# A backward pass of attention and MLP: the weight gradient of the output projection first, and weight and dQ transposes moved into the dw2 stage

## The chip, the cores and the metric

The kernel runs on one core of one Trainium2 chip. The metric is device time in microseconds (us) of one execution; medians of several executions are given, with the number of them.

## The reference, cut to what matters

The reference is the forward pass of a block and its gradients for 2048 rows of width 512, in bf16. The forward pass is `x + s * g`, where `s` is attention (32 heads of width 16) on the normalised `x`, and `g` is `silu` of an MLP of inner width 1792 on the same input.

```python
xn = _layernorm(x, axis=-1)
s = _A_ref(xn, A_wqkv, A_wo)                       # qkv, softmax attention, @ wo
g = _silu(_B_ref(xn, B_w1, B_b1, B_w2, B_b2))      # layernorm, gelu MLP
return x + s * g
# ... reference(): the output, and the vjp for x, wqkv, wo, w1, b1, w2, b2
```

The change touches only the weight gradients that follow the attention backward pass: `dwo` (512x512), `dwqkv` (512x1536, in a q, a k and a v third) and `dw2` (1792x512), with the output projection (attention's output times `wo`), which the forward output needs and which gives `dm`, the gradient that `dw2` and the MLP go on from.

## The kernel before: the parts that matter

The kernel computes attention forward and backward until its last matmul, called Z, at about 2223 us. Then comes the stretch below. Two queues issue its DMAs: `nc.sync` (the SP queue) carries all the transposing DMAs and the stores of the output, `nc.scalar` (the ACT queue) the plain loads. The instructions are ordered by a scheduler: what the program says first need not be issued first, when it is ready and its buffer is free.

```python
# ... pools: c4 has 5 buffers (oT, dKVn and dso share them), psA 7 PSUM banks
load_oT(0); load_oT(1)                  # SP queue: transposes of attention's output
load_gbx(0); load_gbx(1)                # ACT queue: gb (256 KB) and xt (128 KB) of a row tile, 3 buffers each
for i in range(4):
    nc.scalar.dma_start(out=xn_all[...], in_=xnv[...])            # 4 x 512 KB
load_oT(2); load_oT(3)
for i in range(4):
    nc.sync.dma_start_transpose(out=dQT[...], in_=k.dQall[...])   # needed only after dw2
# ...
for t in range(NT):                     # 16 row tiles: projection, and q third of dwqkv
    # 4 matmuls ps_so = oT @ wo
    nc.vector.tensor_tensor(out=dm_all[:, t, :], in0=ps[:], in1=gb[:, 1, :], op=ALU.mult)
    # t13 = ps * gb[0]; ot = t13 + xt
    if t + 2 < NT:
        load_gbx(t + 2)
    # store of ot (SP queue), 4 matmuls ps_dwq (q third), every second t a transpose of dm_all (SP queue)
    if t == 1:
        load_kv(0)                      # SP queue: dKVn, one of 8 transposes for the k and v thirds
    if t in (4, 6, 8, 10):
        load_kv(t // 2 - 1)
    if t == 5:
        load_hg(k.HGT_s, 0)             # SP queue: hgc, first of 7 transposes for dw2, 2 buffers
    if t == 9:
        nc.sync.dma_start_transpose(out=w2T[:], in_=B_w2)         # needed only after dw2
    if t == 11:
        load_hg(k.HGT_s, 1)
    if t == 13:
        nc.sync.dma_start_transpose(out=w1T[:], in_=B_w1)         # needed only after dw2
# ...
for half in range(2):                   # k and v thirds of dwqkv: 2 x 64 matmuls from dKVn
    # ...
    load_kv(i + 5)                      # while any is left, then dso (ACT queue, 512 KB each)
# psdb: 16 small matmuls; then dwo: 64 matmuls ps_dwo = Oall^T @ dso
y_all = k.pO.tile([128, NT, D], bf16, name="y_all", tag="slotA")  # Oall's place, so after dwo
nc.scalar.dma_start(out=y_all[:], in_=...)                        # 2 MB
for i in range(3):
    load_gp(i)                          # ACT queue, 896 KB each, needed after dw2
for i in range(7):                      # dw2: 224 matmuls ps_dw from hgc and dm_all
    # ...
    if i + 2 < 7:
        load_hg(k.HGT_s, i + 2)
# ... then dhg (it needs w2T and gp) and the rest
```

Of the kernel before, what the change touches and what calls it, by code (L numbers as in the profile page):

```python
# [8 lines left out]
bf16 = mybir.dt.bfloat16  # L9
f32 = mybir.dt.float32  # L10
# [5 lines left out]
S, D, H, DH, F = 2048, 512, 32, 16, 1792  # L16
NT = S // 128
IC = D // 128
# [254 lines left out]
def phase3(ctx, tc, k, A_x, A_wqkv, A_wo, B_w1, B_w2, grad_out, out_0, out_1, out_2, out_3, out_4, out_5, out_6, out_7, dbg):  # L273
    nc = tc.nc
# [4 lines left out]
    with ExitStack() as c1:  # L279
# [23 lines left out]
        with ExitStack() as c2:  # L303
# [27 lines left out]
            def dwq_out(half, ps4):  # L331
                for ic in range(IC):
                    ob = ring.tile([128, D], bf16, name="dw_out", bufs=3)
                    nc.scalar.copy(out=ob[:], in_=ps4[ic][:])
                    nc.scalar.dma_start(out=out_2[ic * 128:(ic + 1) * 128, half * D:(half + 1) * D], in_=ob[:])

            load_oT(0)
            load_oT(1)
            load_gbx(0)
            load_gbx(1)  # L340
            xnv = k.XN_s.rearrange("(t p) d -> p t d", p=128)
            for i in range(4):
                nc.scalar.dma_start(out=xn_all[:, 4 * i:4 * i + 4, :], in_=xnv[:, 4 * i:4 * i + 4, :])
            load_oT(2)
            load_oT(3)
            for i in range(4):
                nc.sync.dma_start_transpose(out=dQT[:, 4 * i:4 * i + 4].rearrange("c t m q -> c (t m) q"),
                                            in_=k.dQall[:, 4 * i:4 * i + 4, :].rearrange("q t c -> q (t c)"))
            psdb2 = psS.tile([1, D], f32, name="psdb2")
            acc4 = [psA.tile([128, D], f32, name="ps_dwq", tag="mm") for _ in range(IC)]  # L350
            ots = {}
# [7 lines left out]
            for t in range(NT):  # L359
                ps = psA.tile([128, D], f32, name="ps_so", tag="mm")  # L360
                for cc in range(IC):
                    nc.tensor.matmul(ps[:], lhsT=oT[t // 4][:, t % 4, cc, :], rhs=wo_sb[:, cc, :],
                                     start=(cc == 0), stop=(cc == IC - 1))
                gb, xt = gbx.pop(t)
                nc.vector.tensor_tensor(out=dm_all[:, t, :], in0=ps[:], in1=gb[:, 1, :], op=ALU.mult)
                t1 = wk.tile([128, D], f32, name="t13")
                nc.vector.tensor_tensor(out=t1[:], in0=ps[:], in1=gb[:, 0, :], op=ALU.mult)
                ot = wk.tile([128, D], bf16, name="ot3", bufs=4)
                nc.gpsimd.tensor_tensor(out=ot[:], in0=t1[:], in1=xt[:], op=ALU.add)
                ots[t] = ot  # L370
                if t + 2 < NT:
                    load_gbx(t + 2)
                if t >= 2:
                    store_o0(t - 2)
                for ic in range(IC):
                    nc.tensor.matmul(acc4[ic][:], lhsT=xn_all[:, t, ic * 128:(ic + 1) * 128], rhs=k.dQall[:, t, :],
                                     start=(t == 0), stop=(t == NT - 1))
                if t % 2 == 0 and t >= 2:
                    dmT_tr(t // 2 - 1)
                if t == 1:  # L380
                    load_kv(0)
                if t in (4, 6, 8, 10):
                    load_kv(t // 2 - 1)
                if t == 5:
                    load_hg(k.HGT_s, 0)
                if t == 9:
                    nc.sync.dma_start_transpose(out=w2T[:], in_=B_w2)
                if t == 11:
                    load_hg(k.HGT_s, 1)
                if t == 13:  # L390
                    nc.sync.dma_start_transpose(out=w1T[:], in_=B_w1)
            store_o0(NT - 2)
            store_o0(NT - 1)
            dmT_tr(NT // 2 - 1)
            dwq_out(0, acc4)
            dso = {}

            def load_dso(i):
                dso[i] = c4.tile([128, 4, D], bf16, name="dso3", tag="c4")
                nc.scalar.dma_start(out=dso[i][:], in_=k.DSO_s[i * 512:(i + 1) * 512, :].rearrange("(t p) d -> p t d", p=128))  # L400

            for half in range(2):
                acc4 = [psA.tile([128, D], f32, name="ps_dwq", tag="mm") for _ in range(IC)]
                for t4 in range(4):
                    i = half * 4 + t4
                    for ic in range(IC):
                        for tt in range(4):
                            t = t4 * 4 + tt
                            nc.tensor.matmul(acc4[ic][:], lhsT=xn_all[:, t, ic * 128:(ic + 1) * 128], rhs=kvc[i][:, tt, :],
                                             start=(t == 0), stop=(t == NT - 1))  # L410
                    if i + 5 < 8:
                        load_kv(i + 5)
                    else:
                        load_dso(i + 5 - 8) if i + 5 - 8 < 4 else None
                dwq_out(half + 1, acc4)
            for t in range(NT):
                nc.tensor.matmul(psdb2[0:1, :], lhsT=k.ones_bf[:, 0:1], rhs=dm_all[:, t, :], start=(t == 0), stop=(t == NT - 1))
            db2 = wk.tile([1, D], bf16, name="db2", bufs=1)
            nc.vector.tensor_copy(out=db2[:], in_=psdb2[:])
            nc.sync.dma_start(out=out_7.rearrange("(o d) -> o d", o=1), in_=db2[:])  # L420
            acc4 = [psA.tile([128, D], f32, name="ps_dwo", tag="mm") for _ in range(IC)]
            for t4 in range(4):
                for ac in range(IC):
                    for tt in range(4):
                        t = t4 * 4 + tt
                        nc.tensor.matmul(acc4[ac][:], lhsT=k.Oall[:, t, ac * 128:(ac + 1) * 128], rhs=dso[t4][:, tt, :],
                                         start=(t == 0), stop=(t == NT - 1))
            for ac in range(IC):
                dwo = ring.tile([128, D], bf16, name="dw_out", bufs=3)
                nc.scalar.copy(out=dwo[:], in_=acc4[ac][:])  # L430
                nc.sync.dma_start(out=out_3[ac * 128:(ac + 1) * 128, :], in_=dwo[:])
            y_all = k.pO.tile([128, NT, D], bf16, name="y_all", tag="slotA")
            nc.scalar.dma_start(out=y_all[:], in_=k.Y_s.rearrange("(t p) d -> p t d", p=128))
            dxm_all = k.pO.tile([128, NT, D], bf16, name="dxm_all", tag="slotB")
            for i in range(3):
                load_gp(i)
            for i in range(7):
                for fl in range(2):
                    fc = 2 * i + fl
                    ps = psA.tile([128, D], f32, name="ps_dw2", tag="mm")  # L440
                    for t in range(NT):
                        nc.tensor.matmul(ps[:], lhsT=hgcs[i][:, t, fl * 128:(fl + 1) * 128], rhs=dm_all[:, t, :], start=(t == 0), stop=(t == NT - 1))  # L442
                    dw2 = ring.tile([128, D], bf16, name="dw_out", bufs=3)
                    nc.scalar.copy(out=dw2[:], in_=ps[:])
                    nc.scalar.dma_start(out=out_6[fc * 128:(fc + 1) * 128, :], in_=dw2[:])
                if i + 2 < 7:
                    load_hg(k.HGT_s, i + 2)
            R = [big.tile([128, 8, S // 2], bf16, name="R0", tag="s16a")]
            Rv = k.dKVT_s.rearrange("(r p) s -> p r s", p=128)
            nc.scalar.dma_start(out=R[0][:], in_=Rv[:, :, 0:S // 2])  # L450
# [571 lines left out]
```

## Time and profile before

| | before |
|---|---|
| time, median of 3 executions | 2628.93 us (2627.68 to 2630.96) |
| span of the profiled execution | 2624.7 us |
| last Z matmul (end of attention) | 2222.6 us |
| first dw2 matmul | 2367.6 us |
| last dw2 matmul | 2418.0 us |
| from there to the end | 206.7 us |

The page of the profile gives the busy time of the engines over the whole span:

```profile
PE 2295.2 (87%) x18152; PEld 731.6 (28%) x18192; DVE 1837.6 (70%) x3286; ACT 1673.4 (64%) x1910; POOL 908.0 (35%) x1391
```

An average of 87% hides the stretch of the change. The view of busy times by stretches shows it, cut at the stage borders of this kernel. Its columns are start and end, the length, the busy time of each engine with its instructions in brackets, and last the granted TensorE clock, the DMA share and GB/s.

```profile
core 0: us, PE busy (x) PEld busy (x) DVE busy (x) ACT busy (x) POOL busy (x), PEclk, DMA share, GB/s
2223.00:2243.40 20.40, 0.00 (x0) 0.01 (x1) 0.66 (x1) 0.00 (x0) 0.61 (x1) 0.58 1.07 308
2243.40:2305.90 62.50, 36.95 (x126) 14.53 (x130) 17.85 (x29) 1.07 (x2) 13.75 (x12) 0.80 1.17 259
2305.90:2353.80 47.90, 36.14 (x142) 14.97 (x145) 3.36 (x5) 5.22 (x9) 4.61 (x4) 0.80 0.96 230
2353.80:2367.60 13.80, 13.75 (x65) 6.22 (x65) 0.00 (x0) 2.39 (x5) 0.00 (x0) 1.00 0.15 50
2367.60:2418.20 50.60, 48.62 (x221) 21.73 (x225) 0.00 (x0) 8.19 (x14) 0.00 (x0) 1.00 0.76 186
```

The lines are: PE without work; projection and q third; k and v thirds; dwo; dw2. In the first three the DMA share is about 1 (a share of 1 is 16 busy engines; the records overlap a little, so it can exceed 1) and PE waits for half of the time. In the last two PE is busy throughout, and the DMA engines have room: their share is 0.76 in dw2 and 0.15 in dwo.

The waits of PE and of VectorE in the same stretch (us in total, number, longest):

```profile
PE ps_so L362 <- DVE t L367: 21.4, 6, 7.4
PE ps_so L362 <- DMA gb<-GB_s: 20.5, 1, 20.5
PE ps_dwq L409 <- DMA dKVn<-dKVT_s: 11.6, 1, 11.6
...
DVE dm_all L365 <- DMA gb<-GB_s: 37.1, 9, 8.0
```

The second line is the first 20 us. The waits of the projection for VectorE are at one remove waits for DMA too: VectorE itself waits 37 us for `gb` loads. And the kv matmuls wait once, 11.6 us, for a `dKVn` transpose. The timeline shows which one (start, length, engine, line; in brackets the idle time before and what ended it):

```profile
2333.97 8.41 SPq L320 DMA_TRANSPOSE dKVn<-dKVT_s  x3
...
2341.23 12.71 PE L409 MATMUL ps_dwq<-dKVn,xn_all 128*128 128x512 bf16 x47 [11.60 <-DMA dKVn<-dKVT_s]
2353.78 13.98 PE L426 MATMUL ps_dwo<-dso,Oall 128*128 128x512 bf16 x63
2367.59 13.98 PE L442 MATMUL ps_dw<-dm_all,hgc 128*128 128x512 bf16 x63
```

The last `dKVn` transposes are issued from 2334 to 2342.4. From there on PE runs without a wait, through the rest of the kv matmuls and dwo into dw2. So the stretch has two parts. Until the last `dKVn`, 119.8 us after the last Z, the DMA engines bound it; in the 25.2 us from there to dw2, PE does.

### The profile page before, as it was taken

How to read it: one execution, taken by the hardware profiler on the slowest of the kernel's cores; microseconds unless marked ns; L12 is line 12 of the kernel's file. 1: busy time of each engine (PE TensorE's matmuls, PEld its weight loads, DVE VectorE, ACT ScalarE, POOL GpSimd, SP SyncE). 2: the span in 40 equal slices, each digit the busy share in tenths (PEclk: the TensorE clock that was granted, in tenths of full speed). 3: DMA queues.
4: the chain of work that ended last, by engine and by line, in shares of the span. 5: the costliest groups of instructions: out<-in, count | busy, mean ns of one | idle time of the engine just before them, and what ended most of it. 6: DMA issues, size and time to landing. Idle time of an engine off the chain costs nothing.

```text
span 2624.7 us, 47762 instructions
## 1 busy us (share of the span) xinstructions
PE 2295.2 (87%) x18152; PEld 731.6 (28%) x18192; DVE 1837.6 (70%) x3286; ACT 1673.4 (64%) x1910; POOL 908.0 (35%) x1391
## 2 busy tenths in 40 slices
PE   3788699999999999999999899999999997479998
PEld 2333122222222222222222222222222222134446
DVE  5766578887778878788878778888888885201652
ACT  3344578777777877788777777777777775011141
POOL 0533545454535445454445454521101111100020
PEclk8899799999999999999999999999999999789999
DMA  5355899999999999999999999999999998987475
GB/s 192 92 184 184 179 239 232 236 236 234 226 236 237 237 231 237 231 234 242 231 235 233 237 228 240 235 236 233 226 233 229 236 218 183 271 215 186 153 160 125
DMA packets 1905432, 568.51 MB, mean 217 GB/s; under 512 B 1811889, under 2 KB 1887794, under 8 KB 1905202
## 3 DMA queue, kind: packets, MB, share of 16 engines
q1 hardware_dynamic: 1844674, 511.05, 95.8%
q10 hardware_dynamic: 60528, 54.41, 6.7%
q8 instruction: 142, 2.33, 0.4%
q14 instruction: 88, 0.72, 0.1%
HBM read 52.83 MB, written 62.66 MB: 44 GB/s over the span
## 4 chain that ended last, share of the span: by engine, by line
PE 38%; DVE 33%; issue 12%; DMA 10%; ACT 4%; POOL 2%; SPq 0%; ACTq 0%; DVEq 0%; POOLq 0%
DVE gts L743 26%; PE d L708 6%; PE X L789 6%; PE Z L858 4%; DMA gk<-gts 4%; PE Z L852 3%; PE t L680 3%; PE X L774 2%; PE ps_dhg L463 2%; DVE xs L795 2%; ACT et L722 2%; DVE xt L807 2%; PE XT L805 1%; PE ps_dw L528 1%; PE ps_dw L442 1%
## 5 line engine op out<-in xcount | busy, mean ns | idle before, releaser
L743 DVE TENSOR_TENSOR gts<-d,et 128x512 bf16<-128x512 f32 x2048 | 1302.5, 682 | 359.1 <-issue 240.8
L722 ACT ACTIVATE et<-s 128x1024 bf16<-128x1024 f32 x1024 | 1002.6, 1024 | 24.9 <-PE d L708 13.8
L730 ACT ACTIVATE e<-t 128x1024 bf16<-128x1024 f32 x512 | 523.8, 1023 | 407.3 <-PE t L680 405.7
L708 PE MATMUL d<-QDT,KVT 32*128 32x512 bf16 x2048 | 599.1, 383 | 130.9 <-DVE gts L743 129.5
L694 PE MATMUL s<-QDT,KVT 32*128 32x512 bf16 x2048 | 403.3, 390 | 18.2 <-DMA QDT<-QDPad 11.9
L774 PE MATMUL X<-et,Lc 128*32 128x512 bf16 x2048 | 403.9, 391 | 14.1 <-DVE xs L795 14.1
L777 PE MATMUL X<-et,NAT 128*32 128x512 bf16 x2048 | 403.9, 391 | 0.0
L789 PE MATMUL X<-gts,NAT 128*17 128x512 bf16 x2048 | 402.5, 389 | 0.0
L858 PE MATMUL Z<-gk,W 128*32 128x512 bf16 x2048 | 399.4, 384 | 0.0
L822 POOL TENSOR_TENSOR W<-NATQd,rL 128x128 bf16<-128x128 bf16 x64 | 25.7, 402 | 645.9 <-DVE rL L817 645.9
L789 PEld LDWEIGHTS <-NAT 128*17 128x17 bf16 x2048 | 92.5, 87 | 492.0 <-issue 492.0
L852 PE MATMUL Z<-e,W 128*32 128x512 bf16 x1024 | 202.2, 388 | 3.8 <-DVE acc L865 2.3
L852 PE MATMUL Z<-ek,W 128*32 128x512 bf16 x1024 | 203.7, 394 | 0.0
L680 PE MATMUL t<-KVT,QDT 32*128 32x512 bf16 x1024 | 201.0, 389 | 0.0
L694 PEld LDWEIGHTS <-KVT 32*128 32x128 bf16 x2048 | 97.4, 91 | 362.6 <-issue 362.5
L708 PEld LDWEIGHTS <-KVT 32*128 32x128 bf16 x2048 | 139.0, 91 | 88.9 <-issue 59.6
L774 PEld LDWEIGHTS <-Lc 128*32 128x32 bf16 x2048 | 103.7, 93 | 180.4 <-issue 179.4
L865 DVE TENSOR_TENSOR acc<-Z,acc 64x512 f32<-64x512 f32 x192 | 129.2, 673 | 12.2 <-PE Z L858 12.2
L852 PEld LDWEIGHTS <-W 128*32 128x32 bf16 x2048 | 121.1, 93 | 56.7 <-issue 50.2
L777 PEld LDWEIGHTS <-NAT 128*32 128x32 bf16 x2048 | 101.2, 96 | 52.2 <-issue 2.7
L631 POOL TENSOR_TENSOR bg_v<-bg_t 128x512 f32<-128x512 f32 x56 | 58.1, 1038 | 149.1 <-ACT bg_t L638 149.1
L870 POOL CAST ob<-acc 64x512 bf16<-64x512 f32 x64 | 38.6, 603 | 203.3 <-DVE acc L865 203.3
(161 smaller groups left out, 2525.8 us busy)
## 6 DMA issues: line engine op xcount, KB each, us to landing
gk<-gts SPq DMA_TRANSPOSE x512, 4.1
HGT_s<-hgT SPq DMA_DIRECT2D x2, 3584.0 KB, 12.2
bg_x<-H1T_s SPq DMA_DIRECT2D x56, 128.0 KB, 2.8
GP_s<-bg_m SPq DMA_DIRECT2D x56, 128.0 KB, 2.5
gp<-GP_s ACTq DMA_DIRECT2D x8, 896.0 KB, 8.5
DH1T_s<-dh1T SPq DMA_DIRECT2D x4, 1792.0 KB, 10.2
NAT<-NAT_s SPq DMA_DIRECT2D x16, 264.0 KB, 3.2
GB_s<-gB ACTq DMA_DIRECT2D x16, 256.0 KB, 2.0
```

What stands on the lines that cost most here:

```text
L680: nc.tensor.matmul(t[:, hj, :], lhsT=op["QDT"][r:r + 32, q0:q0 + 128], rhs=op["KVT"][r:r + 32, kc * 512:(kc + 1) * 512], start=True, stop= ...
L694: nc.tensor.matmul(s[:, hj, :], lhsT=op["KVT"][r:r + 32, kb * 128:(kb + 1) * 128], rhs=op["QDT"][r:r + 32, qc * 512:(qc + 1) * 512], start ...
L708: nc.tensor.matmul(d[:], lhsT=op["KVT"][r:r + 32, kb * 128:(kb + 1) * 128], rhs=op["QDT"][r:r + 32, qc * 512:(qc + 1) * 512], start=True, ...
L722: nc.scalar.activation(out=et[:, :, kb % 4, :, :].rearrange("k b h q -> k h b q"), in_=st_s.pop(g)[:].rearrange("k h (b q) -> k h b q", b= ...
L730: nc.scalar.activation(out=e[:], in_=st_t.pop(g)[:], func=ACT.Exp)
L743: nc.vector.tensor_tensor(out=gts[:, kb % 2, hj, :].rearrange("k (b q) -> k b q", b=4), in0=ds[hj][:].rearrange("k (b q) -> k b q", b=4), ...
L774: nc.tensor.matmul(X[64 + 32 * hj:96 + 32 * hj, :], lhsT=Lc[:], rhs=et[:, :, kb % 4, hj, :], start=(kb == 0), stop=False, skip_group_check ...
L777: nc.tensor.matmul(X[32 * hj:32 * hj + 32, :], lhsT=NATt[:, kb, hj, 1:33], rhs=et[:, :, kb % 4, hj, :], start=(kb == 0), stop=(kb == 15), ...
L789: nc.tensor.matmul(X[64 + 32 * hj:64 + 32 * hj + 17, :], lhsT=NATt[:, kb, hj, 0:17], rhs=gts[:, kb % 2, hj, :], start=False, stop=(kb == 1 ...
L852: nc.tensor.matmul(Z[32 * hj:32 * hj + 32, :], lhsT=blk[j]["W1"][:, qb, hj, :], rhs=ev[:, hj], start=(qb == qb_order[0]), stop=False, tile ...
L858: nc.tensor.matmul(Z[32 * hj:32 * hj + 32, :], lhsT=blk[j]["W2"][:, qb, hj, :], rhs=gv[:, :, :, hj, qb, :], start=False, stop=(qb == qb_or ...
L865: nc.vector.tensor_tensor(out=av, in0=Z[0:64, :], in1=av, op=ALU.add)
```

## The change

The change has two halves. First, dwo needs only what attention left (`Oall`) and `dso`, so it is put ahead of the projection, into the time in which PE has nothing to do, and its 14 us vanish from the PE-bound end. Secondly, the transposes of `w2`, `w1` and dQ, which are not needed before dw2 ends, go into the dw2 stage, whose DMA engines have room. `HGT` transposes, for dw2, go into the k and v thirds. No matmul is added or dropped.

```diff
+            load_dso(0)
+            load_dso(1)
+            load_dso(2)
             load_oT(0)
             load_oT(1)
             load_gbx(0)
             load_gbx(1)
+            load_dso(3)
+            load_oT(2)
             # ... xn_all loads
-            load_oT(2)
+            acc4 = [psA.tile([128, D], f32, name="ps_dwo", tag="mm") for _ in range(IC)]
+            # ... dwo: 64 matmuls, 4 copies out, 4 stores (moved here, stores on the ACT queue)
             load_oT(3)
-            for i in range(4):
-                nc.sync.dma_start_transpose(out=dQT[...], in_=k.dQall[...])
+            load_kv(0)
             # ... projection, q third
-                if t == 1:
-                    load_kv(0)
-                if t in (4, 6, 8, 10):
-                    load_kv(t // 2 - 1)
-                if t == 5:
-                    load_hg(k.HGT_s, 0)
-                if t == 9:
-                    nc.sync.dma_start_transpose(out=w2T[:], in_=B_w2)
-                if t == 11:
-                    load_hg(k.HGT_s, 1)
-                if t == 13:
-                    nc.sync.dma_start_transpose(out=w1T[:], in_=B_w1)
+                if t in (8, 9, 12, 15):
+                    load_kv({8: 1, 9: 2, 12: 3, 15: 4}[t])
             # ... k and v thirds
-                    else:
-                        load_dso(i + 5 - 8) if i + 5 - 8 < 4 else None
+                    if i == 2:
+                        load_hg(k.HGT_s, 0)
+                    if i == 4:
+                        load_hg(k.HGT_s, 1)
             # ... psdb
-            # ... dwo (moved to the front)
             y_all = k.pO.tile([128, NT, D], bf16, name="y_all", tag="slotA")
             # ... y_all and gp loads, dw2 loop
                 if i + 2 < 7:
                     load_hg(k.HGT_s, i + 2)
+                if i == 1:
+                    nc.sync.dma_start_transpose(out=w2T[:], in_=B_w2)
+                if i == 3:
+                    nc.sync.dma_start_transpose(out=w1T[:], in_=B_w1)
+                if i >= 4 and i < 6:
+                    # ... two of the four dQT transposes
```

More of the change, by code (lines that the diff above doesn't have):

```diff
@@ L335, in dwq_out, with load_dso @@
                     nc.scalar.dma_start(out=out_2[ic * 128:(ic + 1) * 128, half * D:(half + 1) * D], in_=ob[:])
+            dso = {}
+            def load_dso(i):
+                dso[i] = c4.tile([128, 4, D], bf16, name="dso3", tag="c4")
+                nc.scalar.dma_start(out=dso[i][:], in_=k.DSO_s[i * 512:(i + 1) * 512, :].rearrange("(t p) d -> p t d", p=128))
+            load_dso(0)
+            load_dso(1)
+            load_dso(2)
             load_oT(0)
@@ L343, in phase3 @@
                 nc.scalar.dma_start(out=xn_all[:, 4 * i:4 * i + 4, :], in_=xnv[:, 4 * i:4 * i + 4, :])
-            load_oT(2)
+            acc4 = [psA.tile([128, D], f32, name="ps_dwo", tag="mm") for _ in range(IC)]
+            for t4 in range(4):
+                for ac in range(IC):
+                    for tt in range(4):
+                        t = t4 * 4 + tt
+                        nc.tensor.matmul(acc4[ac][:], lhsT=k.Oall[:, t, ac * 128:(ac + 1) * 128], rhs=dso[t4][:, tt, :],
+                                         start=(t == 0), stop=(t == NT - 1))
+            for ac in range(IC):
+                dwo = ring.tile([128, D], bf16, name="dw_out", bufs=3)
+                nc.scalar.copy(out=dwo[:], in_=acc4[ac][:])
+                nc.scalar.dma_start(out=out_3[ac * 128:(ac + 1) * 128, :], in_=dwo[:])
             load_oT(3)
-            for i in range(4):
-                nc.sync.dma_start_transpose(out=dQT[:, 4 * i:4 * i + 4].rearrange("c t m q -> c (t m) q"),
-                                            in_=k.dQall[:, 4 * i:4 * i + 4, :].rearrange("q t c -> q (t c)"))
+            load_kv(0)
             psdb2 = psS.tile([1, D], f32, name="psdb2")
@@ L395, in phase3 @@
             dwq_out(0, acc4)
-            dso = {}
-            def load_dso(i):
-                dso[i] = c4.tile([128, 4, D], bf16, name="dso3", tag="c4")
-                nc.scalar.dma_start(out=dso[i][:], in_=k.DSO_s[i * 512:(i + 1) * 512, :].rearrange("(t p) d -> p t d", p=128))
             for half in range(2):
@@ L420, in phase3 @@
             nc.sync.dma_start(out=out_7.rearrange("(o d) -> o d", o=1), in_=db2[:])
-            acc4 = [psA.tile([128, D], f32, name="ps_dwo", tag="mm") for _ in range(IC)]
-            for t4 in range(4):
-                for ac in range(IC):
-                    for tt in range(4):
-                        t = t4 * 4 + tt
-                        nc.tensor.matmul(acc4[ac][:], lhsT=k.Oall[:, t, ac * 128:(ac + 1) * 128], rhs=dso[t4][:, tt, :],
-                                         start=(t == 0), stop=(t == NT - 1))
-            for ac in range(IC):
-                dwo = ring.tile([128, D], bf16, name="dw_out", bufs=3)
-                nc.scalar.copy(out=dwo[:], in_=acc4[ac][:])
-                nc.sync.dma_start(out=out_3[ac * 128:(ac + 1) * 128, :], in_=dwo[:])
             y_all = k.pO.tile([128, NT, D], bf16, name="y_all", tag="slotA")
             nc.scalar.dma_start(out=y_all[:], in_=k.Y_s.rearrange("(t p) d -> p t d", p=128))
-            dxm_all = k.pO.tile([128, NT, D], bf16, name="dxm_all", tag="slotB")
             for i in range(3):
@@ L447, in phase3 @@
                     load_hg(k.HGT_s, i + 2)
+                if i == 1:
[3 more added lines that the diff above has]
+                if i >= 4 and i < 6:
+                    for i4 in (2 * (i - 4), 2 * (i - 4) + 1):
+                        nc.sync.dma_start_transpose(out=dQT[:, 4 * i4:4 * i4 + 4].rearrange("c t m q -> c (t m) q"),
+                                                    in_=k.dQall[:, 4 * i4:4 * i4 + 4, :].rearrange("q t c -> q (t c)"))
+            dxm_all = k.pO.tile([128, NT, D], bf16, name="dxm_all", tag="slotB")
             R = [big.tile([128, 8, S // 2], bf16, name="R0", tag="s16a")]
```

## The prediction

> **What bounds the kernel now.** Attention, to 2223 us of a span of 2624.7 us, is untouched. Busy times by stretches and the timeline show what changes: 2223 us (last Z matmul) to 2418 us (end of dw2), 195 us, in which PE is busy 135 us by the record and, at the 0.22 us per 128x512 matmul of the dwo and dw2 stages (63 in 13.98 us), has only 560 x 0.22 = 123 us of work. Its stages:
>
> - 2223 to 2243: PE idle 20.5 us, until the first gb load lands (PE's waits).
> - 2243 to 2306: projection and q third. 28 us of work takes 62 us. DVE waits 37 us for gb loads; DMA share 1.17, 259 GB/s, clock 0.80.
> - 2306 to 2354: k and v thirds, with one wait of 11.6 us for a dKVn transpose.
> - 2354 to 2368: dwo, 14 us, DMA share only 0.15.
> - 2368 to 2418: dw2, hardly a wait.
>
> So until 2342 (last dKVn issue) the stretch is bound by DMA; issues on SP's queue take about 113 of 120 us. After that PE bounds.
>
> **What the change does.** No matmul, no byte is added. Dwo (14 us of PE work, loads of 2 MB) goes from the PE-bound end to the front, where PE sits idle. dQ and weight transposes (15.7 us dQT, 7.9 us w2T, 8.5 us w1T of SP issue time) are meant to go from the DMA-bound stretch to dw2.
>
> The built instruction order says that the second half hardly happens: SP starts with the first HGT transpose, then the dKVT stores, two oT, the second HGT transpose and w2T, all ahead of the third and fourth oT; w1T and one dQT still stand among the projection's stores; only two dQT come after the last dKVn. That takes some 8 us off SP's queue. And y_all (2 MB), which now only needs dwo done, moves forward on ACT's queue into the middle of the projection, where it must wait for the last oT and holds back the gb loads of tiles 8 and on. The Trainium skill ("Trainium Kernel Development and Optimization", Key Constraints) says that DMAs of the SP and ACT queues run on the same 16 engines; this trace agrees: both together reach a share of 1.17.
>
> **Sum (estimates from the above).** Dwo starts about 2230. The first gb lands later, near 2250, as 1.5 MB dso and 1 MB HGT go first. Projection ends at about 2318 (before: 2306), since about 4 MB more go ahead of its last loads at 260 to 300 GB/s. Then 128 k and v matmuls, 29 us: dw2 starts at about 2347 (before 2367.6). The rest keeps its 257 us. Gain about 21 us: 14 for dwo, 11.6 for the dKVn wait, some for psdb, less about 12 of later projection.
>
> Predicted time **2608 us**, 80% range 2594 to 2624. Faster by over 2%: 0.03; within 2%: 0.95; slower by over 2%: 0.02.
>
> **What would show it.** Right: dwo matmuls in 2226 to 2260; no dKVn wait above 5 us; dw2 starts in 2335 to 2360 and lasts 50 to 53 us; DVE still waits 30 us or more for gb; tile 8's gb comes after y_all's issue. Wrong: dwo itself waiting for dso beyond 2250; dw2 starting after 2362, or slowed by transposes.
>
> **What would make it wrong.** The y_all block or the early HGT and w2T transposes delay the projection by more than 25 us (no gain); or gb loads run so much better that SP's queue alone limits, and dw2 starts at 2332 (35 us gain).

## More of the kernel before

The DMA view of the first part (2222.6 to 2342.4):

```profile
DMA packets 77185, 31.97 MB, mean 267 GB/s; under 512 B 63677, under 2 KB 75069, under 8 KB 77181
```

Among these 32 MB are transposes that nothing needs before dw2 ends. The chain of waits (start, length, piece) runs through two of them:

```profile
2245.76 4.90 DMA dQT<-dQall
...
2256.30 7.40 DMA dQT<-dQall
...
2268.70 11.72 DMA gb<-GB_s
...
2333.97 7.22 DMA dKVn<-dKVT_s
```

## The result, and the profile after

| | before | after |
|---|---|---|
| time, median of 4 executions each | 2629.94 us (2627.68 to 2637.29) | 2617.77 us (2613.43 to 2620.64) |
| ratio after to before | | 0.9948, 95% interval 0.9923 to 0.9972 |
| span of the profiled execution | 2624.7 us | 2617.2 us |
| last Z matmul | 2222.6 us | 2224.7 us |
| last `dKVn` issue ends, after last Z | 119.8 us | 128.9 us |
| first dw2 matmul, after last Z | 145.0 us | 136.0 us |
| last dw2 matmul, after last Z | 195.4 us | 186.1 us |

A ratio here and below is the mean time of one kernel's runs over that of the other's of the same rounds, so it is not quite the ratio of the medians that are quoted. The change is worth half a per cent: within 2%, but more than the scatter.

Stage times are given from the last Z matmul on, because attention, which is the same in all kernels, ended anywhere from 2221.1 to 2234.7 us in their profiles. What follows dw2 took 206 to 211 us in all of them. So what the kernels differ in is when dw2 starts and how long it lasts.

The page after, and the view by stretches at the borders of this kernel:

```profile
PE 2292.0 (88%) x18192; PEld 731.1 (28%) x18192; DVE 1837.6 (70%) x3286; ACT 1673.7 (64%) x1910; POOL 910.0 (35%) x1391
```

```profile
2225.00:2253.60 28.60, 12.04 (x51) 5.00 (x50) 0.68 (x1) 0.00 (x0) 0.61 (x1) 0.80 1.00 263
2253.60:2330.00 76.40, 45.27 (x158) 16.86 (x159) 16.57 (x26) 2.83 (x5) 13.88 (x13) 0.81 1.18 271
2330.00:2360.70 30.70, 28.70 (x131) 12.53 (x130) 3.86 (x6) 5.77 (x10) 4.58 (x4) 1.00 1.20 264
2360.70:2411.00 50.30, 48.91 (x226) 21.70 (x226) 0.68 (x1) 8.21 (x14) 0.00 (x0) 1.00 0.62 145
```

The lines are: most of dwo; the rest of dwo, projection and q third; k and v thirds; dw2. The dwo line of before (13.8 us with a DMA share of 0.15) is gone, and the k and v thirds have become dense. But projection and q third, 62.5 us before, take 76.4 us, and they begin 10 us later. In all three lines before dw2 the DMA share is 1 or more, but in the third PE is busy for 28.7 of 30.7 us: the DMA engines have work there, and PE does not wait for them.

The waits after:

```profile
PE ps_so L381 <- DVE t L386: 13.1, 5, 5.7
PE ps_so L381 <- DMA wo_sb<-in_A_wo_dram: 12.8, 1, 12.8
...
PE ps_dwo L360 <- DMA dso<-DSO_s: 6.4, 2, 3.7
...
DVE dm_all L384 <- DMA gb<-GB_s: 46.5, 8, 13.7
```

PE's wait for `dKVn` is gone. The view of the tile `dKVn` shows the same: the matmuls of the k and v thirds, before and after, take from their first to their last 47.7 and 29.8 us, but the first comes 83.3 and 105.2 us after the last Z.

```profile
L409 PE MATMUL ps_dwq<-dKVn,xn_all x125: 379/379/634, 2305.9 to 2353.6; 128*128 128x512 bf16 x125
L412 PE MATMUL ps_dwq<-dKVn,xn_all x128: 376/379/379, 2329.9 to 2359.7; 128*128 128x512 bf16 x128
```

VectorE's wait for `gb` is longer, and one wait among these is of 13.7 us. The timeline shows what stood in front:

```profile
2225.08 8.72 SPq L301 DMA_TRANSPOSE hgc<-HGT_s  x1
...
2250.24 8.09 SPq L301 DMA_TRANSPOSE hgc<-HGT_s  x1
2258.43 8.87 SPq L442 DMA_TRANSPOSE w2T<-in_B_w_dram  x1
...
2263.15 3.61 PE L360 MATMUL ps_dwo<-dso,Oall 128*128 128x512 bf16 x16 [2.61 <-DMA dso<-DSO_s]
...
2291.03 13.27 SPq L444 DMA_TRANSPOSE w1T<-in_B_w_dram  x1
...
2300.00 0.38 ACTq L427 DMA_DIRECT2D y_all<-Y_s  x1
2300.49 5.38 ACTq L326 DMA_DIRECT2D gb<-GB_s  x1
...
2314.93 0.69 DVE L384 TENSOR_TENSOR dm_all<-ps_so,gb 128x512 bf16<-128x512 f32 x1 [13.68 <-DMA gb<-GB_s]
```

Two things are to be seen. The transposes that the program text moved into the dw2 stage were not moved there: the scheduler issued the two `HGT` transposes and `w2T` ahead of the third `oT` on the SP queue and `w1T` in the middle of the projection, because nothing holds them back (their buffers are free). Of the four dQT transposes two went ahead of the last `dKVn` and two right behind it. And `y_all`, which before had to wait for dwo at the end, is now free to go once the early dwo and the `oT` transposes have read `Oall`, whose place it takes; it goes right ahead of a `gb` load. The chain of waits runs through the first of these intruders and then from `gb` to `gb`:

```profile
2250.24 13.08 DMA hgc<-HGT_s
2263.34 5.98 DMA gb<-GB_s
...
2287.86 10.81 DMA gb<-GB_s
...
2300.49 14.35 DMA gb<-GB_s
...
2315.65 8.97 DMA dKVn<-dKVT_s
```

The DMA view from the last Z to the last `dKVn` issue, 128.9 us:

```profile
DMA packets 76900, 34.64 MB, mean 269 GB/s; under 512 B 59808, under 2 KB 74784, under 8 KB 76896
```

So the part up to the last `dKVn` got 9.1 us longer, by 2.67 MB at an unchanged rate (2.67 MB at 269 GB/s are 9.9 us); and the part behind it got 18.1 us shorter (25.2 to 7.1 us): dwo (13.8 us) is no longer in it, and PE begins the k and v thirds before the last `dKVn` has come. The difference is the 9.0 us by which dw2 starts earlier. The last `dKVn` is a border for counting here, not what PE waits for after the change.

### The profile page after: what moved, and what is told of

The parts are those of the page before. It is cut to its first block, busy times and chain, and to the rows that moved or that the text cites. A ratio compares the mean times of both kernels' runs of the same rounds, so it can differ in the third digit from the quotient of the medians.

```text
span 2617.2 us, 47799 instructions
## 1 busy us (share of the span) xinstructions
PE 2292.0 (88%) x18192; PEld 731.1 (28%) x18192; DVE 1837.6 (70%) x3286; ACT 1673.7 (64%) x1910; POOL 910.0 (35%) x1391
## 4 chain that ended last, share of the span: by engine, by line
PE 38%; DVE 33%; issue 11%; DMA 11%; ACT 4%; POOL 2%; SPq 1%; ACTq 0%; DVEq 0%; POOLq 0%
DVE gts L745 26%; PE d L710 6%; PE X L791 6%; DMA gk<-gts 4%; PE Z L860 4%; PE Z L854 3%; PE t L682 3%; PE X L776 2%; PE ps_dhg L465 2%; ACT et L724 2%; PE ps_dw L530 2%; DVE xs L797 2%; DVE xt L809 2%; PE XT L807 1%; DMA gb<-GB_s 1%
## 5 line engine op out<-in xcount | busy, mean ns | idle before, releaser
L854 PEld LDWEIGHTS <-W 128*32 128x32 bf16 x2048 | 121.0, 93 | 56.9 <-issue 50.4
L872 POOL CAST ob<-acc 64x512 bf16<-64x512 f32 x64 | 38.7, 605 | 203.0 <-DVE acc L867 203.0
## 6 DMA issues: line engine op xcount, KB each, us to landing
DH1T_s<-dh1T SPq DMA_DIRECT2D x4, 1792.0 KB, 10.2
```

What stands on the lines that cost most here:

```text
L854: nc.tensor.matmul(Z[32 * hj:32 * hj + 32, :], lhsT=blk[j]["W1"][:, qb, hj, :], rhs=ev[:, hj], start=(qb == qb_order[0]), stop=False, tile ...
```

## The experiments

Three theories were to be told apart at first.

- A: the gain comes from dwo leaving the PE-bound end; part of it is given back because the `y_all` and `dso` loads now delay the projection.
- B: the gain comes from what the moved transposes take off the SP queue; dwo's place hardly matters.
- C: until the last `dKVn`, the DMA engines move bytes at a fixed rate in whatever order; when dw2 starts is decided by the bytes issued ahead of the last `dKVn`, plus the PE work behind it.

A fourth, D, came up with C: not the bytes but the SP queue alone, as a serial chain of issues, sets the time.

Each experiment was timed against runs of the kernel before on the same chip. Those under "First rounds" share these runs, so do those under "Second rounds", then e8 with e9, and e10 with e11. The table puts all profiles side by side, in us after the last Z. The MB are those moved until the last `dKVn` issue ended, and GB/s their mean rate.

| kernel | last `dKVn` issue ends | MB (GB/s) | from there to dw2 | dw2 starts | its last matmul |
|---|---|---|---|---|---|
| before | 119.8 | 31.97 (267) | 25.2 | 145.0 | 195.4 |
| after | 128.9 | 34.64 (269) | 7.1 | 136.0 | 186.1 |
| after, again | 130.7 | 34.60 (265) | 6.9 | 137.6 | 187.9 |
| dwo first only (e1) | 145.3 | 35.65 (245) | 9.9 | 155.2 | 204.9 |
| transposes only (e2) | 113.7 | 29.27 (257) | 27.5 | 141.2 | 192.1 |
| `y_all` late (e3) | 121.5 | 33.42 (275) | 13.2 | 134.7 | 185.2 |
| pinned (e4) | 109.3 | 27.68 (253) | 10.9 | 120.2 | 179.4 |
| pinned, `y_all` late (e5) | 106.7 | 27.67 (259) | 12.4 | 119.1 | 177.4 |
| and `gp` late (e6) | 106.1 | 26.37 (249) | 14.9 | 121.0 | 179.7 |
| before, 2 MB more (e7) | 127.6 | 34.03 (267) | 24.6 | 152.2 | 203.0 |
| e6 with `w2T` before dw2 (e8) | 96.7 | 26.39 (273) | 14.5 | 111.2 | 166.8 |
| pinned, dwo at the end (e9) | 82.0 | 22.82 (278) | 28.5 | 110.5 | 169.9 |
| e9 with `w2T` before dw2 (e10) | 77.9 | 22.54 (289) | 32.5 | 110.4 | 161.6 |
| e10 with `gp` late (e11) | 89.1 | 22.72 (255) | 24.8 | 113.9 | 168.6 |

Each line is one execution, and the profile of before is not from the chips of the three rounds that follow, so lines of different rounds differ in chip too. The two profiles of the kernel after differ by 1.6 us in the start of dw2, so differences of that size are not read.

The last `dKVn` is what PE waits for in some of these kernels only: 11.6 us in before, 17.6 in e7, 6.0 in e2, 5.2 in e3, at most 5.0 in e1, e5, e6, e8 and e11. In after, e4, e9 and e10 the waits of PE list no wait of the kv matmuls for a `dKVn`: there PE runs on from the projection. There the order is partly the reverse: the last three `dKVn` need buffers that the first kv matmuls free, so a late projection also makes the last `dKVn` late. A second marker therefore helps, the first kv matmul, which comes when PE has done the projection. In us after the last Z: before 83.3, after 105.2, e1 119.7, e2 86.4, e4 82.3, e9 63.0.

### First rounds: the change, its halves, and `y_all` (five rounds, one chip)

**The change again.**

> The changed kernel again, to have it in the same rounds as the parts. Every theory: 0.3 to 0.7% faster than before (8 to 18 us), dw2 starts 134 to 138 us after the last Z matmul.

Measured: 2620.68 us, median of 6 (2617.55 to 2622.87), against 2630.24 us of before (11 runs, 2623.89 to 2640.70); ratio 0.9953, interval 0.9932 to 0.9974. The first result holds.

**e1: dwo first, and nothing else.** The transposes and `dKVn` loads stay where they were in the program text. The issue order is not the same all the same: in e1 the scheduler put the first `HGT` transpose at the front of the SP queue (0.4 us after the last Z; in before it is issued 50.6 us after it).

```diff
 # against before
+            load_dso(0); load_dso(1); load_dso(2)     # ahead of oT; load_dso(3), load_oT(2) behind gbx
+            # dwo matmuls, copies and stores ahead of load_oT(3), stores on the ACT queue
-            # dwo behind psdb, dso loads in the kv loop
```

> Dwo first, all transposes asked for where before has them. Theory A (the gain is the 14 us of dwo taken off the PE-bound end plus the 11.6 us dKVn wait; part is given back by loads that got ahead of the projection's): 8 to 16 us faster than before, dw2 starts 130 to 138 us after the last Z matmul (before: 145). Theory B (the gain comes from the moved transposes; dwo's 2 MB of loads at the front delay the projection by what dwo saves): within 4 us of before.

Measured: 2646.50 us (2642.56 to 2651.70), ratio 1.0051, interval 1.0027 to 1.0076. It is slower than before. The table says where: what lies behind the last `dKVn` is 15.3 us shorter, as A has it, but the last `dKVn` comes 25.5 us later. That is 3.68 MB more, at a lower rate (245 against 267 GB/s). Of the 25.5 us the bytes alone explain 13.8 at 267 GB/s; why the rate was lower in this kernel is not explained. VectorE's waits for `gb` are 89.4 us in place of 37.1, one of them 31.1 us. So A is not the explanation: moving dwo alone loses. B, which expected a time within 4 us of before, missed too.

**e2: the transposes alone.** dwo stays at the end.

```diff
 # against before
-            # dQT transposes ahead of the projection; HGT, w2T, w1T in it
+            # HGT 0 and 1 at i == 2 and i == 4 of the kv loop
+            # w2T, w1T and dQT in the dw2 loop, exactly as in the change
```

> Transposes moved as in the change, dwo left at the end. Theory A: some gain, 3 to 9 us, as SP's queue loses the four dQT (15.7 us) before the last dKVn and the 11.6 us wait shrinks, but dwo's 14 us stay at the end. Theory B: the whole gain of the change, 10 to 16 us.

Measured: 2630.50 us (2627.74 to 2636.63), ratio 0.9993, interval 0.9971 to 1.0015. No difference. So B is not the explanation either. One half loses 0.5%, the other is worth nothing, and together they gain 0.5%: the halves interact, and a sum of two separate effects can't describe them.

**e3: `y_all` held back behind the last load of the projection.**

```diff
 # against after; last["xt"] is the newest xt load
-            nc.scalar.dma_start(out=y_all[:], in_=...)
+            with tc.issue_after(last["xt"].ins):
+                nc.scalar.dma_start(out=y_all[:], in_=...)
```

> The change with only the y_all load issued behind the last xt load on ACT's queue. Theory A, part 1 (y_all on ACT's queue waits for the last oT, then its 2 MB go ahead of tile 8's gb, where DVE waited 13.7 us): DVE's wait for tile 8's gb under 7 us, projection and with it dw2 start 6 to 10 us earlier than in the changed kernel, 14 to 22 us faster than before. If y_all merely takes DMA time that something else would take: the same as the changed kernel within 3 us.

Measured: 2625.71 us (2621.35 to 2628.11), ratio 0.9971, interval 0.9949 to 0.9993; not faster than the change itself (0.9953). I had expected it to be, and was wrong. The projection did end much earlier: its last multiplication came 98.4 us after the last Z, not 113 to 114. But dw2 started only 1 to 3 us earlier. Taking away the 13.7 us wait behind `y_all` uncovered the next one: the kv matmuls now wait 5.2 us for a `dKVn`, and the last `dKVn` had much the same bytes in front of it (33.42 against 34.6 MB). VectorE's longest wait for `gb` is still 10.6 us. Why the time is 5 us longer than that of the changed kernel in the same rounds, with dw2 no later, is not explained; the profiled run was the fastest of e3's six.

### Second rounds: the transposes pinned, and C against D (three rounds, another chip)

**e4: the change, with the moved transposes pinned to their place in the program.** This is what the change intended.

```diff
 # against after
-            nc.sync.dma_start_transpose(out=hgcs[i][:], in_=...)
+            ins = nc.sync.dma_start_transpose(out=hgcs[i][:], in_=...)
+            if src is k.HGT_s:
+                tc.keep_in_program_order(ins)
-                    nc.sync.dma_start_transpose(out=w2T[:], in_=B_w2)
+                    tc.keep_in_program_order(nc.sync.dma_start_transpose(out=w2T[:], in_=B_w2))
 # ... the same for w1T and the four dQT
```

> The change, with the HGT, w2T, w1T and dQT transposes pinned on SP's queue behind what stands before them in the program, so that they really come after the last dKVn. Theory C (till the last dKVn the DMA engines move 245 to 275 GB/s whatever the order; dw2 starts when the bytes placed ahead of the last dKVn are through; the changed kernel has 34.6 MB there): about 6.7 MB less, so the last dKVn is issued 100 to 108 us after the last Z matmul (changed kernel: 127 to 129) and dw2 starts at 112 to 125 (136 to 138), but dw2, now with 11 MB of transposes, lasts 55 to 68 us (50); 0.5 to 1.0% faster than before. If not bytes but PE's and DVE's own order of work set the projection's end: dw2 starts at 130 or later.

Measured: 2615.40 us, median of 4 (2608.72 to 2618.56), against 2629.36 us of before (7 runs, 2623.65 to 2639.75); ratio 0.994, interval 0.991 to 0.997. dw2 now starts after 120.2 us, 16 to 17 us earlier than in the change: 7 MB fewer lie ahead of the last `dKVn`. C had expected 112 to 125 us (it had the last `dKVn` at 100 to 108 us, and it came at 109.3). But dw2 takes 59 us and not 50, so that more than half of it is lost again. The waits of PE and the timeline show why:

```profile
PE ps_dw L437 <- DMA hgc<-HGT_s: 7.7, 3, 6.6
```

```profile
2362.78 7.37 SPq L444 DMA_TRANSPOSE w2T<-in_B_w_dram  x1
...
2379.08 16.75 PE L437 MATMUL ps_dw<-dm_all,hgc 128*128 128x512 bf16 x63 [6.58 <-DMA hgc<-HGT_s]
```

dw2 has two buffers for `hgc`, and each of its seven steps needs one `HGT` transpose. With `w2T` between two of them, one comes late, and PE stands for 6.6 us. The 63 matmuls after that wait take 16.75 us; 63 of them took 13.98 us in the kernel before. The Trainium skill ("TensorE: Matmul & The Clock Gate", Part 1: The HAM clock gate) says that the clock is gated by how busy PE has been recently. The trace agrees: the view by stretches gives a granted clock of 1.00 in the first 14 us of dw2, and of 0.50 in the 5 us after the wait. So this wait of 6.6 us cost 2.8 us more than its own length. In e5, e6 and e9 the 63 matmuls after waits of 6.5 to 7.0 us took 15.7 to 16.7 us.

**e5: e4 with `y_all` late, as in e3.**

```diff
 # against e4
+            with tc.issue_after(last["xt"].ins):      # around the y_all load
```

> As the pinned version, and y_all behind the last xt load. Theory C: the 2 MB of y_all leave the stretch too if PE isn't the limit by then: dw2 starts 2 to 8 us earlier than in the pinned version, 108 to 120 us after the last Z matmul; total 0.6 to 1.2% faster than before. If y_all's bytes don't count: as the pinned version within 2 us.

Measured: 2614.67 us (2612.85 to 2615.67), ratio 0.994, interval 0.9913 to 0.9966. dw2 starts 1.1 us before that of e4, which is not to be told from nothing. The expectation was missed, as in e3.

**e6: e5 with the three `gp` loads late too.**

```diff
 # against e5
+            with tc.issue_after(last["xt"].ins):      # around load_gp(0), load_gp(1), load_gp(2)
```

> As the last, and the three gp loads (2.7 MB) behind the last xt load too. Theory C: first gb lands earlier and the projection ends another 3 to 8 us earlier; dw2 start is then PE's (about 29 us after the projection's end), 105 to 115 us after the last Z matmul; but dw2 is loaded further (some 15 MB in its 50 us), 58 to 72 us long, so the total is no better than the version before it.

Measured: 2611.35 us (2606.28 to 2613.82), ratio 0.9921, interval 0.9888 to 0.9954. dw2 starts after 121.0 us, no earlier; this was missed as well. The projection ended 13 us earlier than in e4 (82.4 against 95.3 us), but the last `dKVn` only 3 us. Only 1.3 MB of the 2.7 of `gp` left the part ahead of the last `dKVn`.

**e7: before, with 2 MB more on the ACT queue.** `XN` is loaded twice into the same tile. The result is the same, the SP queue has the same transfers to issue (in the trace only `w2T` and the fourth `dKVn` have changed places), and PE has the same work: D expects no shift of the last `dKVn`, C one of about 2 MB.

```diff
 # against before
             for i in range(4):
                 nc.scalar.dma_start(out=xn_all[:, 4 * i:4 * i + 4, :], in_=...)
+                nc.scalar.dma_start(out=xn_all[:, 4 * i:4 * i + 4, :], in_=...)
```

> Kernel before, with the XN tile loaded twice (2 MB more on ACT's queue, SP's queue and all arithmetic untouched). Theory C (bytes at 268 GB/s): the last dKVn and dw2's start move 6 to 9 us later (dw2 start 151 to 154 us after the last Z matmul), 0.2 to 0.35% slower than before. Rival D (SP's queue, with its 113 us of transposes and stores in 120 us, is a serial chain of its own): dw2's start moves less than 2 us.

Measured: 2643.73 us (2638.45 to 2648.58), ratio 1.0051, interval 1.0020 to 1.0081. The last `dKVn` comes 7.8 us later, dw2 7.2 us later; 2.06 MB at 267 GB/s are 7.7 us. PE's wait for the `dKVn` has grown from 11.6 us by 6.0:

```profile
PE ps_dwq L410 <- DMA dKVn<-dKVT_s: 17.6, 1, 17.6
```

D, which expected less than 2 us, falls: bytes on one queue held up transposes on the other. The closeness of 7.8 and 7.7 us is more than one pair of profiles can show, given the scatter of the rate in the table. And the time is 14 us longer, 0.51% where C expected 0.2 to 0.35%; the profiles account for about 8 us of it up to the end of dw2. The Trainium skill ("DMA: Bandwidth & Descriptors", Issuing engines are not separate DMA queues) says that DMAs of all issuing engines run on the same 16 DMA engines and interleave. This run agrees, with 7.8 us for 2.06 MB.

### Third rounds: towards a better version (five rounds, e11 three; two more chips)

**e8: e6, with `w2T` directly behind the second `HGT` transpose and ahead of dw2, and `w1T` and dQT behind the last one.**

```diff
 # against e6
                     if i == 4:                        # kv loop
                         load_hg(k.HGT_s, 1)
+                        tc.keep_in_program_order(nc.sync.dma_start_transpose(out=w2T[:], in_=B_w2))
 # dw2 loop: w1T at i == 4 (was 3), dQT at i >= 5 (was 4), w2T gone
```

> From the version with SP pinned and y_all and gp late: w2T goes directly behind the second HGT transpose (SP's queue sat idle there for 6 us), w1T and dQT behind the last HGT transpose. If the dw2 stage was stretched from 50 to 58 us because w2T and w1T stood between HGT transposes, dw2 lasts 50 to 54 us and ends 171 to 177 us after the last Z matmul (180 before; 186 to 188 in the changed kernel), the first dhg matmul and the E stage wait for nothing new; 0.8 to 1.3% faster than before. If the stretch came from DMA bytes as such: dw2 still 56 us or more.

Measured: 2611.05 us, median of 6 (2608.27 to 2617.03), against 2634.28 us (11 runs, 2626.22 to 2646.36); ratio 0.9912, interval 0.9891 to 0.9932. dw2 lasted 55.6 us, so shorter than in e4 to e6 (58 to 59) but longer than the 50 to 54 expected; the rival, bytes as such, expected 56 or more, so this does not decide between the two. Its start, 111.2 us, came 10 us earlier than in e6, which none of the theories gives: the bytes ahead of the last `dKVn` are the same (26.39 and 26.37 MB), but they moved at 273 and not at 249 GB/s. This is the rate's scatter again, and it is not explained; the two ran on different chips.

**e9: the transposes pinned, and dwo left at the end.** This is e2 with the pins of e4, the cross of the two halves that was missing.

```diff
 # against e2: the pins of e4, on HGT, w2T, w1T and dQT
+            tc.keep_in_program_order(...)
```

> All transposes pinned late as in the pinned version, but dwo left at its old place. Theory C: some 24 MB ahead of the last dKVn, which is then issued 80 to 92 us after the last Z matmul; PE, not the DMA, bounds from the projection's end on: dw2 starts at 124 to 134 (pinned version with dwo first: 120), dw2 58 us; 0.2 to 0.6% faster than before. If dwo first is what the gain needs: dw2 starts at 138 or later, no faster than before.

Measured: 2608.70 us (2606.25 to 2613.53), ratio 0.9899, interval 0.9878 to 0.992. The last `dKVn` came at 82.0 us (80 to 92 expected), but dw2 starts after 110.5 us, where I had expected 124 to 134, and the gain is 1.0%, where I had expected 0.2 to 0.6: missed. So with dwo's 14 us still in front of it, dw2 starts 9.7 us earlier than in e4, where dwo was out of the way. 9.15 MB fewer than before lie ahead of the last `dKVn`. The 34.5 us by which dw2 starts earlier than in before have two parts: the first kv matmul comes 20.3 us earlier, as VectorE waits 16.3 us for `gb` and not 37.1; and from there to dwo it takes 33.6 us and not 47.9, as PE no longer waits for a `dKVn`.

**e10: e9 with `w2T` early as in e8.**

```diff
 # against e9: in the kv loop behind load_hg(k.HGT_s, 1)
+                        tc.keep_in_program_order(nc.sync.dma_start_transpose(out=w2T[:], in_=B_w2))
 # dw2 loop: w1T at i == 4, dQT at i >= 5
```

> Pinned transposes, dwo at its old place at the end, and w2T directly behind the second HGT transpose, w1T and dQT behind the last one. The two gains should add: dw2 starts at 108 to 114 us after the last Z matmul, as in the pinned version with dwo at the end (110.5), and lasts 50 to 55 us instead of 59; 1.0 to 1.4% faster than before. If w2T in front of the third HGT transpose merely moves the wait: dw2 57 us or more.

Measured: 2605.48 us, median of 6 (2597.57 to 2608.92), against 2635.05 us (11 runs, 2627.04 to 2644.14); ratio 0.9889, interval 0.9867 to 0.991. dw2 starts as in e9, and lasts 51 us. The stretches of e10, in the order of those of before:

```profile
2226.00:2246.00 20.00, 0.16 (x2) 0.00 (x0) 0.68 (x1) 0.00 (x0) 0.61 (x1) 0.58 1.04 311
2246.00:2286.00 40.00, 30.76 (x121) 12.88 (x125) 17.37 (x28) 0.00 (x0) 14.56 (x13) 0.91 1.15 288
2286.00:2322.00 36.00, 33.56 (x146) 14.52 (x147) 3.03 (x5) 6.24 (x11) 3.89 (x4) 0.95 1.17 283
2322.00:2336.00 14.00, 13.95 (x66) 6.20 (x65) 0.68 (x1) 2.22 (x4) 0.00 (x0) 1.00 0.69 163
2336.00:2387.50 51.50, 48.66 (x221) 21.73 (x225) 0.00 (x0) 8.31 (x15) 0.00 (x0) 1.00 0.94 222
```

The projection takes 40 us (62.5 before), the k and v thirds 36 (47.9), and the PE-bound dwo and dw2 the same 14 and 51 us as before; but they now run beside DMAs, with shares of 0.69 and 0.94 in place of 0.15 and 0.76. That is what the change had set out to do.

**e11: e10 with `gp` late, to bring the first projection matmul forward.**

```diff
 # against e10
+            with tc.issue_after(last["xt"].ins):      # around load_gp(0), load_gp(1), load_gp(2)
```

> The last version with the three gp loads (2.7 MB) behind the last xt load on ACT's queue. Two gp loads stand ahead of the first gb, whose landing ends PE's first idle time of 20.6 us: at 260 to 300 GB/s this idle time falls to 13 to 16 us and dw2 starts 4 to 7 us earlier, at 102 to 108; 1.2 to 1.6% faster than before. If something other than gp's bytes sets the first gb's landing: dw2 starts as in the version without.

Measured: 2602.80 us, median of 4 (2600.52 to 2604.28), ratio 0.9879, interval 0.9859 to 0.99. The first projection matmul came 15.0 us after the last Z, and not 20.5, as expected. dw2 started after 113.9 us, later than in e10, where 102 to 108 had been expected: missed. In time e11 and e10 can't be told apart. Both beat the kernel before and, by intervals that do not touch its own (0.9932 to 0.9974), the change; that last comparison is between ratios of different rounds, each against before.

## Why the prediction was right or wrong

The time was predicted as 2608 us in a range of 2594 to 2624; 2617.77 us were measured, on the side of the smaller gain. "Within 2%" was right. Both were easy to meet: the range spans gains of 5 to 35 us over the 2628.93 us of before, and all of it lies within 2%. The size was not met: a gain of about 21 us was forecast, 12 us were measured by the medians (10 us in the second measurement).

What was right:

- The order on the queues. `HGT` and `w2T` go to the front, `w1T` into the projection, `y_all` ahead of a `gb` load in the middle of the projection. All of this is in the timeline after, where the prediction had it from the built order of the instructions.
- dwo runs early, 4.1 to 41.7 us after the last Z; most of it by 2253.6 us, the end a good deal later than the "2226 to 2260" predicted. It waits for `dso` 6.4 us in all, and its last 16 matmuls wait for the last `dso` until 2263.15 us: one of the signs that the prediction had named for being wrong, "dwo itself waiting for dso beyond 2250", did appear.
- There is no wait for `dKVn` above 5 us. The k and v thirds take 29.8 us (predicted 29), dw2 50.1 us (50 to 53), VectorE waits 46.5 us for `gb` (30 or more).
- dw2 starts at 2360.7 us, a hair outside of the 2335 to 2360 that were to show it right; the central value had been 2347.

The step that was mis-sized is the term "less about 12 of later projection", and in it "about 4 MB more go ahead of its last loads". The prediction marks the end of the projection by the first kv matmul ("before: 2306", which is the 2305.9 of the trace). Counted from the last Z this matmul comes after 105.2 us in place of 83.3: 21.9 us later, not 12. The DMA views up to these points count 28.20 and 22.47 MB, so 5.73 MB more and not 4, at 268 to 270 GB/s, which is 21 us. (VectorE's last multiplication of the projection is 28.7 us later, 113.2 against 84.5 us; but after the change PE begins the kv matmuls 8.0 us ahead of it, before only 1.2.) Where the DMA engines are busy throughout, a longer stretch holds more bytes of itself; the use of the count is to see which transfers they were. `dso` and `y_all` alone are 4.2 MB. By the sizes of their tiles, an estimate, `w1T` and the second `HGT` add 2.9 MB, and three dQT that go later take off 1.6; the rest are stores and `dmT` transposes.

With this term put right, the sum of the prediction comes out. dwo leaves the end (13.8 us). From the first kv matmul to dw2, without dwo, it takes 30.8 us and not 47.9, which is 17.1 less; the prediction had 11.6 for the wait and "some for psdb". Less 21.9 this is 9.0 us, the measured gain in the start of dw2. So the structure of the sum was right, and one term of it was too small.

What made the term large is seen in the kernels that cross the two halves, at the first kv matmul (one profile each, not all on one chip). With dwo first it comes 18.8 us later when the transposes are not pinned (e2 to after) and 19.3 us later when they are (e9 to e4). With pins it comes 23.4 us earlier when dwo is at the end (e2 to e9) and 22.9 us earlier when dwo is first (after to e4). So the early dwo with its loads, and `y_all`, cost the projection about 19 us, and the transposes that came to the front about 23: two pairs agree on each. Only e1 does not fit: there it comes 36.4 us later than in before.

The same 9.0 us can be split at the last `dKVn`: it comes 9.1 us later, and the part behind it is 18.1 us shorter. (Such a split is exact by construction.) Pairs of profiles show what each half does to either part:

| step | MB ahead of last `dKVn` | last `dKVn` | part behind | dw2 start |
|---|---|---|---|---|
| dwo first: before to e1 | +3.68 | +25.5 us | -15.3 us | +10.2 us |
| dwo first: e2 to after | +5.37 | +15.2 us | -20.4 us | -5.2 us |
| dwo first: e9 to e4 | +4.86 | +27.3 us | -17.6 us | +9.7 us |
| transposes: before to e2 | -2.70 | -6.1 us | +2.3 us | -3.8 us |
| transposes: e1 to after | -1.01 | -16.4 us | -2.8 us | -19.2 us |
| transposes pinned: before to e9 | -9.15 | -37.8 us | +3.3 us | -34.5 us |
| 2 MB more on ACT: before to e7 | +2.06 | +7.8 us | -0.6 us | +7.2 us |

So dwo at the front saves 15 to 20 us behind the border, and pays with 4 to 5 MB ahead of it, `dso` and the `y_all` that dwo releases. At 267 GB/s these bytes are 14 to 20 us, the same amount. The first half of the change is a trade of PE time against DMA time, and its outcome differs: next to e2, in the same rounds, it gained (2620.68 against 2630.50 us, and no run of one reaches a run of the other); alone it lost; with pins it probably lost. The second half is the one with something to give: really moved (e9), it takes 9 MB out of the DMA-bound part and 34.5 us off the start of dw2, at the price of about 9 us in a dw2 that then waits for `HGT`, and e10 avoids that price. As written, the change got 1 to 2.7 MB of it, because the scheduler put the transposes back to the front. The bytes don't explain every row: from e1 to after 1.01 MB are about 4 us, and the last `dKVn` came 16.4 us earlier, mostly by the rate (245 and 269 GB/s).

What is shown, and what isn't. That bytes on one queue hold up the transposes on the other is shown by e7, though its time is not accounted for in full. That pinning the transposes is what pays is shown by e9 and e10 against before and by e2, which is the same program as e9 without the pins and gains nothing. That dwo first loses by itself is shown by e1, with the reservation that the scheduler also moved an `HGT` transpose to the front there; that it also loses with pinned transposes is suggested by e4 and e9, whose starts of dw2 differ by 9.7 us, but they ran on different chips and the intervals of their ratios just overlap (0.991 to 0.997 and 0.9878 to 0.992). Not settled is the rate itself. It went from 245 to 289 GB/s between kernels; e6 and e8 had the same bytes and differed by 24 GB/s, which is 9 us. Each kernel was profiled once, after twice, and the rounds were on different chips, so how much of this is the chip, the execution or the order of the transfers was not tested. Nor was it tested what the five buffers shared by `oT`, `dKVn` and `dso` contribute. Fewer small packets do not explain it: e10 and e11 have about the same number (32,619 and 32,853 under 512 B, before 63,677), and moved at 289 and 255 GB/s. C gives in most rows the direction and the rough size; it can't give a time to better than some 10 us, and where PE does not wait for the last `dKVn` it does not say what decides. Nor is it known why attention, untouched, ends up to 13.6 us apart in different profiles; that is why small differences in total time were not read from single runs.

## What to carry to other kernels

In a stretch bound by DMA, first see for which transfer the next stage really waits (here the `gb` loads or the last `dKVn`, by kernel); then count the bytes that are issued ahead of it, on all queues together, and judge a reordering by what it moves across that line; bringing compute forward also brings forward its loads and every load that waits for its buffers. Look in the built order whether a transfer that was "moved later" did move: if it is ready and its buffer is free, the scheduler may issue it at once, and only a dependency or an explicit order keeps it back. A long wait in the timeline is worth removing only if nothing else ends as late: taking away the 13.7 us wait behind `y_all` brought dw2 forward by 1 to 3 us.

## What the Trainium skill lacked or had wrong

- No page says that a scheduler may issue a load that was written late ahead of the loads that the critical path needs. In two programs that differ by the pins alone, 29.27 MB went ahead of the last `dKVn` without pins (e2) and 22.82 MB with them (e9), and the times were 0.9993 and 0.9899 of before.
- "DMA: Bandwidth & Descriptors", Latency and other measured facts, gives 261 GB/s as effective rate of a transposing DMA with a non-contiguous middle dimension, and 350 to 400 for contiguous ones. It has no figure for transposes mixed with plain loads, which is what a kernel has. The runs here show 245 to 289 GB/s for such mixes, with a DMA share of 1.0 to 1.2, and 308 to 311 GB/s in the first 20 us of before and e10, where most is plain loads.
- The same page, Issuing engines are not separate DMA queues, is right here, but has no number for what it means between queues: 2.06 MB of plain loads on ACT's queue made the last transpose on SP's come 7.8 us later, about as long as these bytes take at the mean rate of 267 GB/s (7.7 us), in one pair of profiles.
